# The second batch's q on float16 pairs instead of fp32, with the instruction orders planned anew

## The chip, the cores and the metric

The kernel runs on one core of a Trainium2 chip. A core has TensorE (matmuls, called PE in the profile, with its weight loads as PEld), VectorE (DVE), ScalarE (ACT), GpSimd (POOL) and SyncE (SP), which here issues the DMAs. Each engine works through its own queue of instructions and waits on semaphores for the others. The metric is the device time of one execution in microseconds, as a median of several runs.

## The reference

Four batches of eight heads go through an attention with random features; the result, as 2304 tokens of 512, goes through two feed-forward blocks. Cut to what is computed:

```python
# q, k, v: (4, 8, 576, 64), omega: (128, 64); q and k scaled by 64 ** -0.25
def phi(x):                       # 128 features of a row
    h = x @ omega.T - sum(x * x) / 2
    return exp(h - max(h)) / sqrt(128)
q_p, k_p = phi(q_s), phi(k_s)
kv = einsum('bhsm,bhsd->bhmd', k_p, v);  z = sum(k_p, axis=2)
num = einsum('bhsm,bhmd->bhsd', q_p, kv); den = einsum('bhsm,bhm->bhs', q_p, z) + 1e-6
x = (num / den)                   # as (2304, 512)
h = x @ w_in                      # 512 -> 2048
x = (h * sigmoid(1.702 * h)) @ w_out          # 2048 -> 512
out = ((x @ w_a) * (x @ w_b)) @ w_out2        # 512 -> 1536 -> 512
```

## The kernel before

**Numbers.** Most products are made from pairs of float16: a number is split into a high part (a scaled copy, ScalarE) and a low part (scaled number minus high part, VectorE), and a product is three f16 matmuls (high by high, high by low, low by high) added up in PSUM. The alternative is an fp32 matmul, which the trace shows as two records.

**Stages.** The tokens are cut into tiles of 512, one for each batch, and a fifth tile of what is left. The attention of batch 0 runs first, alone (0 to about 55 us, called the front below). Then comes the first feed-forward block, ffn1: for each of five tiles 16 column blocks `h` (L932-934, 12 matmuls of 512 columns), a gate (tanh on ScalarE, L941, or Silu; VectorE L944 and L954; ScalarE L953), and the products with w_out, `y` (L967-969). The attention of batch 1 is woven into ffn1 of tile 0, that of batch 2 into ffn1 of tile 1, and that of batch 3 into tile 2's and 3's. The first gate of tile t is called th`t`_0; in the profiled execution it stands at 65.08 us for tile 0, 180.31 us for tile 1, 274.17 us for tile 2. From about 500 us on ffn2 runs.

**Attention of one head pair.** For k and for q: rows are loaded (L625, L629), transposed, multiplied by omega (`project`), the row sums of squares are taken (ScalarE, L700), and the exponential is taken on ScalarE (L724) after a maximum on VectorE (L758). In batch 0 the transposition is on TensorE (L658, L662), and the transposed tiles `xt` and `xm` are copied out of PSUM by L667 (VectorE) or L669 (ScalarE), chosen by `EVX`. In later batches the rows are split to f16 (`x16`, L680 on ScalarE, L681 on VectorE) and transposed by DMA. Then k's features are multiplied by v to `kv`. In batches 0 and 1 this is fp32, with a copy by ScalarE (L822).

**The features of q.** In `qphase` they have to be transposed once more before they meet `kv`. With `f32=True` (batches 0 and 1 before) nine fp32 transposes on TensorE (L839) go to PSUM, ScalarE copies them out (L841), and ten fp32 products follow (L846). With `f32=False` (batches 2 and 3) the features are split to f16 pairs (`e16`, L734 on ScalarE, L735 on VectorE), one DMA transposition per head pair (L852) makes `eqT`, and 30 f16 products follow (L862-864), with `kv` as a pair too (`kv_parts`, L782 its low part). The result is normalised (L871-876) and becomes the next x tile: in batch 0 by TensorE transposes and two casts (L900 ScalarE, L901 VectorE), later by split and DMA transposition.

**Weights.** The 34 chunks of 1 MB of all weights come as raw 64-bit words, `wraw0` to `wraw33` (L478, on SyncE). VectorE puts each together in three passes (L492, L532, L540), makes sums for ffn2's chunks (L526), ScalarE makes the high parts (L550), VectorE the low ones (L499). This runs beside ffn1.

**Order.** The program is written as generators that are stepped in turn, but the final order on TensorE, VectorE, ScalarE and SyncE is the table `ORDER`, a compressed list of positions for each of the four engines. Where a DMA waits in SyncE's queue, all later ones wait with it.

Forty-five matmuls on a tile `idle` (L1403) are fillers with no result.

Of the kernel before, what the change touches and what calls it, by code (L numbers as in the profile page):

```python
# [25 lines left out]
S_KV = 2.0**2  # L26
# [7 lines left out]
    "eNqt3buua9uyGNZf2bjxCdjrRVKZASsXYMCJoMBwpMROBCeG/12ztyLn2ufeK8OBgz2x15ocfIxeg4tsVb3q//6X//Qf/+U//PWf"  # L34
    "H//46/zjr/jHX/mPv+off/U//pp//PX8x1+vf/z1/vnV/fXPX5yfvzk/f3Xu3/3c/vwccH6OOD+HnJ9j4ud2ce/n5+/j5+/j5+/j"
    "/v3PsfFzbPwcGz/H5s/t8ud2eR/w53b5c7v8uV3+3C5/bpc/t8uf29XP7erndvVzu7rP7Od29XO7+rld/dyufm5XP7frn9v1z+36"
    "53ZzH7vvA/Z9xL4P2e/7HO6Tm/vs7k36Pr35+dH35f7c/N6wf+77HnVvf29+b/38+fPz/vnntvNz27nn5uf28/P383PM/Pzu+XPb"
    "573tzx0/f273/Lnd8+d2z3sSf27z+vn96+f3r5/fv35+//r5/evn96+f37/uWb63+bmf98/t3j+3e//c7v1zu/fP7d4/t3v/3O79"
# [272 lines left out]
def fused_kernel(  # L311
# [13 lines left out]
    nc = tc.nc  # L325
# [4 lines left out]
    P = 128  # L330
# [1222 lines left out]
```

## Time and profile before

| | us |
|---|---|
| median of 3 runs | 876.65 (875.93 to 878.49) |
| profiled execution | 876.83 |
| its span | 874.9 |
| TensorE busy | 862.9 (99%) |
| weight loads | 628.8 (72%) |
| VectorE | 671.0 (77%) |
| ScalarE | 456.1 (52%) |

The span is the stretch of the profiled execution from its first to its last instruction; the execution's own time is 1.9 us longer. Shares are averages over stages that differ. TensorE's records overlap, so that a run of short ones is read by the distance of their starts and not by their drawn lengths.

### The profile page before, as it was taken

Reading aid. Unit: us, or ns where it says so; the run is one execution under the profiler, and the core shown is the slowest. Engines: PE = TensorE matmul, PEld = TensorE weight load, DVE = VectorE, ACT = ScalarE, POOL = GpSimd, SP = SyncE. Lnnn points to the kernel's source line nnn. Section 1 sums busy time; section 2 is a strip of 40 time slices with the busy share of each in tenths; the row PEclk is TensorE's granted clock in tenths of the full one; section 3 lists DMA queues with packets and bytes.
Section 4 is the critical chain, followed back from the end, with each engine's and each line's share of the span. In section 5 each row is a group of like instructions: output and inputs, shape, how many; then the busy total and the mean of one; then the engine's idle time right before and its main releaser. Section 6 shows DMA issues by size and latency. Waiting matters only on the chain.

```text
span 874.9 us, 17363 instructions
## 1 busy us (share of the span) xinstructions
PE 862.9 (99%) x7094; PEld 628.8 (72%) x7094; DVE 671.0 (77%) x1212; ACT 456.1 (52%) x1088; POOL 1.4 (0%) x10
## 2 busy tenths in 40 slices
PE   8999999999999999999999999999999999999997
PEld 6865655645555555544458888889988889888896
DVE  4889999999977877799211389978999558556756
ACT  6787785787667776564232554454543213233221
POOL 0000000000000000000000000000000000000000
PEclk9999999999999999999999999999999999999999
DMA  7947896673766215647110035422432112223312
GB/s 194 256 133 218 203 225 187 181 178 104 189 143 147 35 35 99 146 147 274 49 49 2 25 133 181 150 51 85 147 120 85 25 21 92 78 108 122 79 50 73
DMA packets 129343, 105.35 MB, mean 120 GB/s; under 512 B 97776, under 2 KB 111088, under 8 KB 127216
## 3 DMA queue, kind: packets, MB, share of 16 engines
q1 hardware_dynamic: 128558, 103.66, 41.8%
q8 instruction: 55, 0.90, 0.4%
q10 hardware_dynamic: 706, 0.59, 0.2%
q14 instruction: 24, 0.20, 0.1%
HBM read 71.07 MB, written 17.69 MB: 101 GB/s over the span
## 4 chain that ended last, share of the span: by engine, by line
PE 81%; DVE 10%; ACT 3%; issue 1%; DMA 1%; SPq 0%; ACTq 0%; DVEq 0%
PE y L968 6%; PE y L967 6%; PE y L969 6%; PE ph L932 6%; PE ph L934 6%; PE ph L933 6%; PE oA L1187 3%; PE oA L1189 3%; PE oA L1188 3%; PE paA L1091 3%; PE pbA L1091 3%; PE paA L1092 3%; PE pbA L1092 3%; PE pbA L1093 3%; PE paA L1093 3%; DVE wf L540 2%
## 5 line engine op out<-in xcount | busy, mean ns | idle before, releaser
L968 PE MATMUL y<-gl,w_out 128*128 128x512 f16 (+1 forms) x320 | 114.4, 358 | 0.7 <-DVE gl L954 0.7
L969 PE MATMUL y<-gh,w_out 128*128 128x512 f16 (+1 forms) x320 | 114.4, 358 | 0.0
L967 PE MATMUL y<-gh,w_out 128*128 128x512 f16 (+1 forms) x320 | 112.3, 358 | 0.0
L954 DVE SCALAR_TENSOR_TENSOR gl<-th,gh 128x512 f16<-128x512 f32 (+1 forms) x80 | 50.4, 633 | 67.8 <-ACT gh L953 67.6
L932 PE MATMUL ph<-xT,w_in 128*128 128x512 f16 x256 | 97.0, 379 | 1.4 <-ACT xT L900 0.8
L933 PE MATMUL ph<-xT,w_in 128*128 128x512 f16 x256 | 97.0, 379 | 0.9 <-DVE xT L901 0.9
L934 PE MATMUL ph<-xT,w_in 128*128 128x512 f16 x256 | 97.0, 379 | 0.3 <-DVE w_in L499 0.3
L1091 PE MATMUL paA<-forms,w_a 128*128 128x256 f16 (+1 forms) x240 | 61.0, 262 | 0.5 <-DVE ca L1112 0.5
L1091 PE MATMUL pbA<-forms,w_b 128*128 128x256 f16 (+1 forms) x240 | 61.2, 262 | 0.0
L1093 PE MATMUL pbA<-forms,w_b 128*128 128x256 f16 (+1 forms) x240 | 61.2, 262 | 0.0
L1092 PE MATMUL pbA<-forms,w_b 128*128 128x256 f16 (+1 forms) x240 | 61.1, 262 | 0.0
L1092 PE MATMUL paA<-forms,w_a 128*128 128x256 f16 (+1 forms) x240 | 61.0, 262 | 0.0
L1093 PE MATMUL paA<-forms,w_a 128*128 128x256 f16 (+1 forms) x240 | 61.0, 262 | 0.0
L1187 PE MATMUL oA<-w_o,ab 128*128 128x256 f16 x216 | 58.9, 273 | 0.3 <-DVE o L1195 0.3
L1189 PE MATMUL oA<-w_o,ab 128*128 128x256 f16 x216 | 58.9, 273 | 0.0
L1188 PE MATMUL oA<-w_o,ab 128*128 128x256 f16 x216 | 58.9, 273 | 0.0
L1101 ACT COPY ka<-paA 128x512 f32<-128x512 f32 (+1 forms) x30 | 16.3, 545 | 79.4 <-PE paA L1093 79.4
L953 ACT ACTIVATE gh<-th 128x512 f16<-128x512 f32 (+1 forms) x80 | 47.1, 589 | 14.8 <-DVE th L944 13.7
L1195 DVE SCALAR_TENSOR_TENSOR o<-oA,o 128x512 f32<-128x512 f32 (+1 forms) x45 | 28.4, 632 | 33.3 <-PE oA L1189 33.3
L934 PEld LDWEIGHTS <-w_in 128*128 128x128 f16 x320 | 31.3, 98 | 28.9 <-issue 1.2
L969 PEld LDWEIGHTS <-w_out 128*128 128x128 f16 x320 | 31.4, 98 | 28.8 <-issue 1.2
L933 PEld LDWEIGHTS <-w_in 128*128 128x128 f16 x320 | 31.4, 98 | 28.4 <-issue 1.4
(211 smaller groups left out, 2371.4 us busy)
## 6 DMA issues: line engine op xcount, KB each, us to landing
wraw<-in_moe_w_out_dram SPq DMA_DIRECT2D x14, 1024.0 KB
forms<-fd SPq DMA_DIRECT2D x8, 1792.0 KB
wraw<-in_moe_w_in_dram SPq DMA_DIRECT2D x8, 1024.0 KB
fd<-forms SPq DMA_DIRECT2D x4, 1792.0 KB
wraw<-in_moe_w_a_dram SPq DMA_DIRECT2D x6, 1024.0 KB
wraw<-in_moe_w_b_dram SPq DMA_DIRECT2D x6, 1024.0 KB
vt<-in_v_dram SPq DMA_DIRECT2D x16, 256.0 KB
rawq<-in_q_dram SPq DMA_DIRECT2D x16, 256.0 KB
```

Source lines behind the costliest of these rows:

```text
L932: nc.tensor.matmul(ph[:, :n], w[:, 0, c, fs], xh(c), start=(c == 0), stop=False)
L933: nc.tensor.matmul(ph[:, :n], w[:, 0, c, fs], xl(c), start=False, stop=False)
L934: nc.tensor.matmul(ph[:, :n], w[:, 1, c, fs], xh(c), start=False, stop=(c == KC - 1))
L967: nc.tensor.matmul(o, w[:, 0, f % 4, cs], gh[f][:, :n], start=(f == 0), stop=False)
L968: nc.tensor.matmul(o, w[:, 0, f % 4, cs], gl[f][:, :n], start=False, stop=False)
L969: nc.tensor.matmul(o, w[:, 1, f % 4, cs], gh[f][:, :n], start=False, stop=(f == FC1 - 1))
L1091: nc.tensor.matmul(o[:, i], wh, xh, start=first, stop=False, skip_group_check=True)
L1092: nc.tensor.matmul(o[:, i], wh, xl, start=False, stop=False, skip_group_check=True)
L1093: own["pe"] = nc.tensor.matmul(o[:, i], wl, xh, start=False, stop=final, skip_group_check=True).ins
L1187: nc.tensor.matmul(bank[:, t], lh, wh, start=first, stop=False, skip_group_check=True)
L1188: nc.tensor.matmul(bank[:, t], lh, wl, start=False, stop=False, skip_group_check=True)
L1189: nc.tensor.matmul(bank[:, t], ll, wh, start=False, stop=final, skip_group_check=True)
```

## The change

The code differs in five small places, beside the table.

```diff
@@ constants
-    VT, FILL, EVX = 4, 40, "q"
+    VT, FILL, EVX = 4, 40, ('k0_0', 'k0_1')
@@ features
-                if nm[0] in EVX:
+                if nm in EVX:
                     own["xt", nm] = nc.vector.tensor_scalar(out=o, in0=i, scalar1=S_QK, ...)
                 else:
                     own["xt", nm] = nc.scalar.activation(out=o, in_=i, func=AF.Copy, scale=S_QK)
@@ kphase32, fp32 branch
-        nc.scalar.copy(own["kv"][:, hp], pk)
+        if b:
+            kv_parts(hp, pk, S_KV)
+        else:
+            nc.scalar.copy(own["kv"][:, hp], pk)
@@ qphase, fp32 branch
-                cp = nc.vector.tensor_copy if gi in EVD else nc.scalar.copy
+                cp = nc.vector.tensor_copy if nm in EVD else nc.scalar.copy
@@ front
         for hp in range(2, NHP):
             a_load(att, "k", 0, hp)
+        w_load(0)
         w_steps(START_W, NW1)
@@ batches 1 to 3
-            begin_q(b, att, x1, psp_att, t0 + NHP * AL, AL, b == 1)
+            begin_q(b, att, x1, psp_att, t0 + NHP * AL, AL, False)
@@ ORDER (280 lines of base64)
-    "eNqt3buua9uyGNZf2bjxCdjrRVKZASsXYMCJoMBwpMROBCeG/12ztyLn2ufeK8OBgz2x15ocfIxeg4tsVb3q//6X//Qf/+U//PWf"
+    "eNpdu3uOK9uyINZf2bj2MTjjRVKeALXfgAA5jTYEWe1ITkOOoH9XzRFkrb1vXxmHp3YVk4/MyFzkiJgR/8+//ef/9G//01//5fGv"
```

So in batch 1 q's features are split to f16 pairs and transposed by DMA; k stays fp32, and its result is made a pair. The `EVX` edit moves batch 0's copies of four q tiles (`xt` and `xm`) from VectorE to ScalarE, and those of `k0_0` and `k0_1` from ScalarE to VectorE. `EVD` is empty, so that edit changes nothing. The load of chunk 0 of the weights goes in SyncE's queue ahead of q's rows of batch 0 instead of behind them. Below, line numbers of the changed kernel stand one to four above those of the kernel before.

TensorE, the first products of the second batch's q (`q1_0`), behind the projections of its last head pair (`xt_q1_3`), in the kernel before:

```order
L693 LDWEIGHTS xt_q1_3_1517
L693 MATMUL pa_1660<-om_l_94,xt_q1_3_1517 128x128
L846 MATMUL pa_1699<-kv32_128,eT32_q1_0_1579 128x65 x5
L967 LDWEIGHTS w_out2_91
L967 MATMUL y0_0_1009<-gh0_10_1904,w_out2_91 128x512
```

and now:

```order
L693 LDWEIGHTS xt_q1_3_1526
L693 MATMUL pa_1664<-om_h_93,xt_q1_3_1526 128x128
L866 LDWEIGHTS eqT_q1_0_1595
L866 MATMUL pa_1704<-kvh_97,eqT_q1_0_1595 128x65
L867 LDWEIGHTS eqT_q1_0_1595
L867 MATMUL pa_1704<-kvl_98,eqT_q1_0_1595 128x65
L868 LDWEIGHTS eqT_q1_0_1595
L868 MATMUL pa_1704<-kvh_97,eqT_q1_0_1595 128x65
```

The five fp32 products of one head have become f16 products, three for each.

VectorE, the last instructions ahead of tile 1's first gate, before (`wf` are weight chunks being put together, `w_a0` a finished one of ffn2, `k2` rows of batch 2):

```order
L526 TENSOR_TENSOR sx17_3458<-wf17_2815,sx17_3458 128x256
L532 SCALAR_TENSOR_TENSOR wf18_3545<-wraw18_2614,wf18_3545 128x1024
L710 TENSOR_REDUCE sq_k2_0_2237<-rawk_2_0_1212 128x9
L681 SCALAR_TENSOR_TENSOR x16_k2_1_2264<-rawk_2_1_1326,x16_k2_1_2264 128x9x64
L797 SCALAR_TENSOR_TENSOR v16_k2_1_2618<-vm_134,v16_k2_1_2618 128x2x65
L681 SCALAR_TENSOR_TENSOR x16_k2_2_2322<-rawk_2_2_1440,x16_k2_2_2322 128x9x64
L710 TENSOR_REDUCE sq_k2_1_2269<-rawk_2_1_1326 128x9
L499 SCALAR_TENSOR_TENSOR w_a0_2610<-wf17_2815,w_a0_2610 128x512
L499 SCALAR_TENSOR_TENSOR w_a0_2610<-wf17_2815,w_a0_2610 128x256
L499 SCALAR_TENSOR_TENSOR w_a0_2610<-sx17_3458,w_a0_2610 128x1024
```

and now:

```order
L493 TENSOR_SCALAR wf16_2313<-wraw16_2174 128x1024
L909 TENSOR_TENSOR x16_q1_3x_2118<-xf_q1_3_2029,x16_q1_3x_2118 128x512
L493 TENSOR_SCALAR wf17_2879<-wraw17_2202 128x1024
L911 TENSOR_TENSOR x16r_96<-xf_q1_3_2029,x16r_96 64x128
L798 SCALAR_TENSOR_TENSOR v16_k2_0_2537<-vm_134,v16_k2_0_2537 128x2x65
L682 SCALAR_TENSOR_TENSOR x16_k2_0_2296<-rawk_2_0_1213,x16_k2_0_2296 128x9x64
L798 SCALAR_TENSOR_TENSOR v16_k2_1_2682<-vm_134,v16_k2_1_2682 128x2x65
L798 SCALAR_TENSOR_TENSOR v16_k2_1_2682<-vt_133,v16_k2_1_2682 128x2x260
L711 TENSOR_REDUCE sq_k2_0_2301<-rawk_2_0_1213 128x9
L533 SCALAR_TENSOR_TENSOR wf16_2313<-wraw16_2174,wf16_2313 128x1024
```

Before, chunk 17 was split and 18 half put together here; now it is chunk 16 that is half put together, and 17 has only begun.

ScalarE, around the last casts of the first x tile (`xT0`) and the first gate `th0_0`, before:

```order
L680 ACTIVATE x16_k1_2_972<-rawk_1_2_820 128x9x64
L900 CAST xT0_100<-pa_729 128x512
L680 ACTIVATE x16_k1_3_1062<-rawk_1_3_823 128x9x64
L906 CAST x16r_96<-xf_q0_3_738 64x128
L900 CAST xT0_100<-pa_761 128x512
L724 ACTIVATE e32_k1_0_855<-pa_923,nb_k1_0_1_949 128x128 x4
L550 ACTIVATE w_in0_87<-wf2_841 128x4x256
L941 ACTIVATE th0_0_914<-ph0_0_844 128x512
```

and now:

```order
L904 CAST xT0_100<-pa_763 128x512
L681 ACTIVATE x16_k1_2_972<-rawk_1_2_820 128x9x64
L701 ACTIVATE rawk_1_1_817,sq_k1_1_910<-rawk_1_1_817 128x64 x2
L945 ACTIVATE th0_0_914<-ph0_0_844 128x512
L945 ACTIVATE th0_1_939<-ph0_1_862 128x512
L551 ACTIVATE w_in0_87<-wf4_921 128x4x256
L957 ACTIVATE gh0_0_917<-th0_0_914 128x512
L957 ACTIVATE gh0_1_942<-th0_1_939 128x512
L725 ACTIVATE e32_k1_0_855<-pa_923,nb_k1_0_1_949 128x128 x4
L945 ACTIVATE th0_2_981<-ph0_2_885 128x512
L681 ACTIVATE x16_k1_3_1062<-rawk_1_3_823 128x9x64
```

The splits of batch 1's k rows, `x16_k1_2` and `x16_k1_3`, stood ahead of a cast each; now the last cast is ahead of both, and `x16_k1_3` comes after the third gate.

## Rows read from the trace of the kernel before

**Rows 1.** Page, part 1: engine, busy us, share of the span, instructions.
```profile
PE 862.9 (99%) x7094; PEld 628.8 (72%) x7094; DVE 671.0 (77%) x1212; ACT 456.1 (52%) x1088; POOL 1.4 (0%) x10
```

**Rows 2.** Stretches: length, busy PE, PEld, DVE, ACT, POOL; clock, DMA share, GB/s.
```profile
0.00:20.00 20.00, 17.31 (x124) 13.48 (x125) 9.26 (x25) 12.79 (x35) 1.38 (x10) 0.91 0.71 181
...
60.00:80.00 20.00, 19.14 (x110) 9.46 (x110) 19.84 (x36) 15.58 (x57) 0.00 (x0) 1.00 0.55 154
80.00:100.00 20.00, 20.00 (x137) 12.25 (x137) 19.97 (x32) 15.10 (x56) 0.00 (x0) 1.00 1.04 259
...
240.00:260.00 20.00, 20.00 (x171) 11.07 (x170) 14.32 (x40) 13.73 (x39) 0.00 (x0) 1.00 0.71 153
```

**Rows 3.** Timeline of PE in batch 1's stage: start us, drawn us, instruction.
```profile
130.60 1.23 PE L846 MATMUL pa<-kv,eT_q 128*128 128x65 f32 x10
131.66 0.38 PE L969 MATMUL y<-gh,w_out 128*128 128x512 f16 x1
131.88 0.38 PE L967 MATMUL y<-gh,w_out 128*128 128x512 f16 x1
```

**Rows 4.** Timeline of PE elsewhere, then PEld's group of the f16 products' loads.
```profile
43.01 1.04 PE L839 MATMUL pa<-ident,e_q 128*128 128x128 f32 x8
43.88 0.93 PE L1403 MATMUL idle<-om_h 128*128 128x256 f16 x7
...
258.91 0.19 PE L862 MATMUL pa<-kvh,eqT_q 128*128 128x65 f16 x1
...
259.78 0.20 PE L864 MATMUL pa<-kvh,eqT_q 128*128 128x65 f16 x1
...
L863 PEld LDWEIGHTS <-eqT_q 128*128 128x128 f16 x80 | 7.4, 98 | 1.0 <-issue 0.4
```

**Rows 5.** Groups by line and form, VectorE: busy us, mean ns | idle before.
```profile
L532 DVE SCALAR_TENSOR_TENSOR wf<-wraw,wf 128x1024 int32<-128x1024 int32 x34 | 41.3, 1215 | 0.2
L492 DVE TENSOR_SCALAR wf<-wraw 128x1024 int32<-128x1024 int32 x34 | 23.3, 684 | 1.4 <-DMA wraw<-in_moe_w_in_dram 1.1
L526 DVE TENSOR_TENSOR sx<-wf 128x256 f32<-128x256 f32 x36 | 14.1, 416 | 0.1
L735 DVE SCALAR_TENSOR_TENSOR e_q<-e_q,e_q 128x512 f16<-128x512 f32 x16 | 11.0, 686 | 1.2 <-ACT e_q L734 1.2
L499 DVE SCALAR_TENSOR_TENSOR w_a<-sx,w_a 128x1024 f16<-128x1024 f32 x6 | 7.3, 1218 | 0.0
L782 DVE SCALAR_TENSOR_TENSOR kvl<-pa,kvh 128x130 f16<-128x130 f32 x8 | 2.3, 285 | 0.0
L735 DVE SCALAR_TENSOR_TENSOR e_q<-e_q,e_q 128x128 f16<-128x128 f32 x8 | 2.1, 268 | 0.0
```

**Rows 6.** The same view of ScalarE.
```profile
L734 ACT ACTIVATE e_q<-e_q 128x512 f16<-128x512 f32 x16 | 10.3, 643 | 1.8 <-PE pa L808 1.8
L841 ACT COPY eT_q<-pa 128x512 f32<-128x512 f32 x16 | 9.2, 586 | 5.4 <-PE pa L839 5.4
L669 ACT ACTIVATE xt_k<-pa 128x512 f32<-128x512 f32 x4 | 2.5, 613 | 0.7 <-PE pa L658 0.6
```

**Rows 7.** Waits of PE (us, times, longest), then ScalarE's timeline with [idle before].
```profile
PE ph L933 <- DVE xT L901: 0.9, 1, 0.9
PE ph L932 <- ACT xT L900: 0.8, 1, 0.8
...
59.89 0.68 ACT L680 ACTIVATE x_k<-rawk 128x576 f16<-128x576 f32 x1 [1.17 <-DMA rawk<-in_k_dram]
```

**Rows 8.** One DMA transposition of q in SyncE's timeline, and the stretch around it.
```profile
252.73 3.29 SPq L852 DMA_TRANSPOSE eqT_q<-e_q  x1
...
252.50:256.50 4.00, 4.00 (x27) 1.90 (x24) 3.60 (x9) 2.48 (x6) 0.00 (x0) 1.00 0.81 122
```

**Rows 9.** The first q rows: asked for by SyncE, transposed by PE (timelines).
```profile
12.43 0.60 SPq L625 DMA_DIRECT2D rawq<-in_q_dram  x1
...
19.62 0.61 PE L658 MATMUL pa<-ident,rawq 128*128 128x128 f32 x4
```

More of the change, by code (lines that the diff above doesn't have):

```diff
@@ L33 @@
 ORDER = (
-    "eNqt3buua9uyGNZf2bjxCdjrRVKZASsXYMCJoMBwpMROBCeG/12ztyLn2ufeK8OBgz2x15ocfIxeg4tsVb3q//6X//Qf/+U//PWf"
[L35 to L38, printed above, removed]
@@ L219 @@
[L219 to L222 removed]
+    "eNp13buOK9uyINZf2bj2MTjjRVKeALXfgAA5jTYEWe1ITkOOoH9XzRFkrb1vXxmHp3YVk4/MyFzkiJgR/8+//ef/9G//01//5fGv"
@@ new lines @@
+    "v86//op//ZX/+qv+9Vf/66/511/Pf/31+tdf758/3T///OL8/Ob8/Or8/C5+7n/u/342ip+/x882+bNp/Nwvfu4XP/eLn/vlz9/y"
+    "5355H/zn0c/9373f3e7n5/j5Oe+2P9vlz3b5s13e5+z7mPfB+j5a34fr+7xzn2zuq537EHMfYzzx3WLuFnO3mLvF3C2ed4vn3eL5"
+    "s0X9/Ff9/Efdn+/b/dmsfravn43qZ+v62a5+Nuuf+/XP/frnfv1zv/65z33G+5ruq7mvo3+2ff5sd1/i827z87/Xzzb35b1+trkv"
+    "7r62+9LuK7sv7L6u+7Luq9oXdd/B876D530HTzvwvoPnfQf3YeN138F94Hjd93wf+r6Vu+Xd8G73ui/lHrSfje7dz+Pn5t77PH5u"
+    "Xj/3ev389XWP6b3Hz6O+f+7w/nnM98/f3z+P9P65z/vnUd4/93v/3O99D76jfw/zo+7NDYLHPYKPvjc3Hh43IB73fsJEfNwAOTcq"
@@ new lines @@
+    "zoaJm/taHP17+M89vkdQiaoUSvevN5DOjY5zQ+PcWDrh8e6db1idG1PnBtTZiLr3u4f03GN6SoT53d3iBtdJP92HKv/pUe6D3mg4"
+    "5Q/3dyXy7u/uoT/32J978M890ueGwLnH/9wDfsTk3bNxd37c/Rsvoe8P96FuAJwbAeeGwLkxcG4QnBsFp93FyXWf7UbFuSFxnja7"
+    "h/oepLhHKd7+88bKPVBxj9S5B/vcCDkO+Y2Q45g//afT9d7Fa7kPdZ7+atv7qp7Oave7T3nfzLlv5ngzDrwnfzjL75PfOAhH/8bJ"
+    "uYFy3q4JN1Bv0J37Ss99pee+0nNfadzYiBsH4YJxPJTnuDvsxlA8XFXuwzv3b2zEjY24IRXhmuEP934uM64zLjSuQDfWwnXFheUG"
+    "TdxQiRtckS449w8uUzcs4oZF3LCIGzlRrkf3r+V395FvRMTb/e5/3qCJGzRxAy5uNEW5SrkGOlB327fLn+vfvQDePZl3J+bdiXl3"
@@ new lines @@
+    "Yt6dmPbBDbO4YRY3wqL94V4L737Ju1/yuIzeR7n7L+/+y/s+0rXTxTPc3M3uLsm7D9LV1WXYddiFeK/E936utfcd5X1Hed9R3h2R"
+    "d0dkeXiPcp/jHpk8frpPdI9M3iOT93jkPQAZrvMewL8G934uq3cflH1wz5m80Z73rKiHC/J9jhvtOX6y7b3f3fd5z5m8gZk3MPMG"
+    "ZrY/eND7h3tG5Xjk9/3dvaLfHVsPT34v6Hcn1nHpv9d+e+2ePXnPnrxnT93dVHc3VbrLfYD9F8nNvfM9j/Ie6Wxv5r7me9yy/St2"
+    "H7S9vrvFPQfzns55T7q853Teky6fnty/d/f13aNQ9yiUo3BP4rwncd5TstI/U366O+w+b93nLc97z+l8+52/3nfuzdyXUfdl1N3j"
+    "dXdY2WF339fd2XWfqF5+8s/d/bftHoq6D1oe1Cu4+77s+3ti59vz3vfx9rv7Pm7I1w3MuoFZN1TqhkrdUKnjr/dl3FApofL2z/x9"
@@ new lines @@
+    "Xv8ev/zDe+9393Pfo9r3MPY9jH0PYz/8wQP41/s+243xujFeN0TrngF1z4C6Z0Af/4Lff8K9NP/o3/Du45/z+wf/eQ93373bNyz6"
+    "Hvi+B77vkel7ZDrd727mo8Dd2X13dvs0cPdz3/3cdz+3TwZ3P/d+Xrhb3Gjv+97KZw4fOPaTx33NThIfPG7Il48e98j0PQB9933d"
+    "RynnzPjPu9n4yHI3E/c34OoGXL98RrmvyqF1QH32uUFYT5927qPcICxBeM+F2o8wdzfdI133SPf9aR4++9wPL/egzD0o8/CfPgi9"
+    "7yeex73x2educXfxiIO3m/tsN1RKqLx9xhJ1NnOk77Z73O6+8rsbPn3Dp48/3C1u+HT4YHaf6J61c8/auYdxHKgbFn3Dom9Y9A2L"
+    "vq++PXw4oPdRShw4Mt6gm/sGbfH2Ac7N/cONjblHa+7Rmnu05h6tuUdr7nk597ycGyDjw+INkLkBMjdA5h6F8UR3F48dew/t3KM1"
@@ new lines @@
+    "Lx8N74PeQzY+Rb7cxYu87+M+ed8n7/vk7UOqUPEx1efUGxt9Y6NvbPSNjb6x0Tc2WmzcOGifHI9PoOfe3A+Tx+/ux8m775/2/Q2V"
+    "vqHST//ps+59UKHyEqce4H4AvsfoeY/R8x6jp2N0j37fo/+8r/55T/bnPbee99x6lg+w9ynvWfYs97uPd8/L5432133Q133QV/hA"
+    "ez9Zh7/6wHsf9L7V532rT5+rfbC+b/XpM7K36n28HdX7Fm789Y2/EX9C7yFs76G4b2bu88593rnPOyE6Bdw9vg8Pej923/983ch5"
+    "hf+8H7JvrL1urD3v23/ew/18+919ffbG21/v67th9rqv9OWVelX3EjR3N73uC395oqeP7353d0n53d0v9yi87lF43Xh53Xh53bf6"
+    "8pRvn/Z93L+f9x9ey/2riL1HYe6+n3tk5u77KVF8/3CvZnOvZnOvZnOvZuMrje80+6XmvlJfa8of7mb3KMw9CnOPwtz3Nvcgz33N"
@@ new lines @@
+    "77uf33f/ve9V5f3wu/uV415QXjdKXuUn7/K+wRvjrxvez/uHpz/4duO43b02dzfN3U3z9DXrvqC7m+bpZHJnO8fpd7d4++lucffG"
+    "vJ2hvpr5bnZjyL66mz0d7vtyn/flPu/LfXq592R/3ZP91b6D2e0OwP2db1M3mt5OjYeb+47upeB1w+Lly9c96d73pHu93Ngb99uX"
+    "O+93tvumfWu7J+zbCes0CN8F70u78fe88fe88fcUfwIunXT3zaQvjXeLdNLdLdJ5ee939/PzhsXTzr7v7dm+Xt773ff29EX3xsbz"
+    "xsbzxsbzxsZznJL3qB4v8sZa+mJ5f5feoJ/uLrlP+U77xU/3rd4gfLs8+BZ7j+DzHsHnPYLPewSfrjQ3xp++AN9j+fS19+V7793i"
+    "7qb3PWHf94R936h7u6q8nHn3D+UP96WVL733Fdy4et+4et8d8b479n137Pvu2Pfdse+7Y993x77Dc9z7pXd5D+MNkNcNkNcNkNcN"
@@ new lines @@
+    "kJcAeQhWLHCP+T14r3vwXndvvI4r3N3i7ojXDZXXfdCXB73772X/3SPzvkfmfY/Mu/3O1/W77d27r/TTfRTXjbtPX3efvu4+fd03"
+    "/SoQcJ+3RKwAvve7x/I9Hvm+y/3P+3j3+L5gxv3r6x7fl6vy/vU+2z33X/e0f93T/nVP+9c97d/3kL1fXvPda/eJ3gLkPsD7PvL7"
+    "PvL7Psr7PsrbZuN+9xXch3rfi8f7nuLve4q/7yn+fgIKW9w73wB5L1bcn26AvG+AvG+AvG+AvJ1RL6ZBKx4LJFzjwUhckJxfgoSL"
+    "ODfJCBpxNsMRX3ofqx/LH491Eg9LOx5nH5aaLJYsngCRB9940JAH5nicvXVPLPLgIg+e8gAqD6LyACSP2EdzHyjygCQPNvLAKQ9E"
+    "8gAgj9z7eMbce/q59v6enW88WMlj9vcen3Y8ahnIYzKWB914gIQHU3j03nqE9oyM44FjHuzlMStJ/Oextxho9yeReDz3Z4/ANx5r"
@@ new lines @@
+    "WoTjsaxFLB7I4sEsHrWv3G3ta/YIVOeBdR5c5wF2Hr3vwj2BzAPBPOjJg8Q8gMkDyDyIx2NNbGOAfKC2s0z2IS3H7mNhjt1q2HLY"
+    "Y/YWiD32louJlhWgx8tzIZylmlWbFZv1sTWlRaW1syWzJbT1svWzx4b9a1+5d/f2LKjm8d53Z0++94js+/LKl/XW8BbxVvGW8dbx"
+    "7KVlq/WtVSSMdBaiVqKWotai0NKhLmfRaNVo2ejsK3nvu7CtCF/9WzBcBFwFXAZc7lvvW/Bb7FvtW+5bK1wsXC1cLlwbXDVcE1wU"
+    "XBVcFlwXXBhcGVwVxEYn9mdnAbw+GOZwmMNRDqc5oObkcua+L1stLzLvA70P9T7Y+3DvA74P+T7o+7DvA7YO2Tqx4rlxJbaXF1cG"
+    "1y8B5lmFXIZchzwbmbPbbux5Pbm3XpX9ia8Oqzq5MfPcW4/5WhD2mM7ZVcZlRop2MNrBb4d0HdR1cuPNWba+CBjPCuPKJJU8WPJw"
@@ new lines @@
+    "ybMwCRYPWTxo8bDFAyFPbNZCJHPIAx0PdTzY8XDHAx5PLGavZjt/Y3V6j6z3i3QO0zlQ53ClQ91OLGTv0Re3uXj92j3g914P1zuo"
+    "7UDCQwkPQToI6TCkE6vhq+OiKBbJ9xk/nO51Ojsg5eGaB2wesnm45QGXh0MeynNyZV1EIanDpA6UOrDyoKDDgg4MOjTo4KCDeA7j"
+    "OQDwEMBTe9RctWRqjlTNkas5kjVHtuZI1xz5kRP7ru1nKZITG5P2vyzJid2fXq1EyYl9tRtvrkiU/mD6w+nPQj1oP7FXJHsASx54"
+    "dZjVqc1PvPd2kw5u7UlqcwDdIXQH0R0yd2oTCI4mnDt07uC5g7QOIzuQ7NC5g+dO7bvYPXz21rt47+1mSLyX956VziB7Gzqf/ORY"
+    "HBGPD2wPsT3I9tTe2le471C5ww4PZTuY7YC6Q+oOOzxo8SC/w/wOUDpE6RDJg/IOyzsw79C803u+b5pmr1quM7lJmr3OuFYA6pN7"
@@ L223 @@
+    "bx/ePrx9ePvw9uHtw9uHtw9vH94+vH14+/D24e3D24e3D28f3j68fXj78Pbh7cPbh7cPbx/ePrx9ePvw9uHtw9uHtw9vH94+vH14"
     "+/D24e3D24e3D28f3j68fXj78Pbh7cPbh7cPbx/ePrx9ePvw9uHtw9uHtw9vH94+vH14+/D24e3D24e3D28f3j68fXj78Pbh7cPb"
@@ L307 @@
+    "TQH4HPrJLPgkOt8EwvPD9t8cg08q9eV+Xzl6kwQ+vjw+CYTXJ3nw3mTCN9fi35DYHMm3Jtm/5/1bypufQuG9oDw+6Yn38x8lvflb"
+    "HezsddpGfjMRn+j6LVeefxTefq45v2W+j28Ww+F1RvdvqsCFyLnrMuQq5CLkGrRphvwtKn7+Vha/v/kH16E/GQYn9J+K4a0J/i3Q"
+    "dWlxHXFJcS35U9zrQvLvq4Ofv/of/8gS/Kn//ZMW2OLeb1rgY/5f0N9ryvO3KtkF5T8sEX59EwRbGPz4WP5eHJi12HJMHcrV/y/t"
+    "bwpANS/f/1Pw+6euV3biP6rmdUr+R7XDW2P8+Eq/U865tifgN08R8fyv/+//B4bH+ag="
 )
```

481 lines of the change are left out of this document (218 added, 263 removed).

## The prediction

> **What bounds the kernel now.** I read the page's totals first [rows 1]. TensorE's matmuls cover 99% of the span, its weight loads 72%, VectorE 77% and ScalarE 52%. A row of matmuls can be covered and still stall, since their drawn durations overlap, so the second view is the table by stretches [rows 2]. From 60 to 100 us, where the change's second batch is worked on, two engines are full together: VectorE 19.8 and 20.0 us of 20, TensorE 19.1 and 20.0 us, while weight loads fall to 9.5 and 12.3. Which of them sets the pace is told by the step from one matmul to the next in the timeline of the same stage [rows 3]: a 512-column matmul begins 0.22 us after the one before it, and 512 columns at the granted clock of 1.00, the 2.4 GHz level, are 0.213 us. There is no gap between steps there. TensorE is the bound, and VectorE runs along just full. The reader should take from this that work removed from TensorE's queue shortens the kernel one for one, provided VectorE's queue shrinks as much in the same stage. The third view, the waits, shows what else may be won: few waits of TensorE are near 1 us, two of them on the casts of the first x tile [rows 7].
>
> **TensorE's work.** The second batch's q is four head pairs. Before, each has ten fp32 products. The timeline has ten records, five products, between 130.60 and 131.66 [rows 3], so 1.06 us for five; the four pairs hold eight such fives, 8 x 1.06 = 8.5 us. Each pair also has nine fp32 transposes; eight of them run from 43.01 to 43.88 [rows 4], 0.109 us each, so 36 are 3.9 us. Both go. In their place stand 30 f16 products per pair, 120 in all. The third batch's, which have this form already, begin at 258.91 and the thirtieth at 259.78 [rows 4]: 0.87 us for 29 steps, 0.030 us each, 3.6 us for 120. The sum is 8.5 + 3.9 - 3.6 = 8.8 us less on TensorE. In the order shown, the five fp32 products become a run of f16 products at the same place, directly behind the projections of the fourth head pair, so nothing else is opened up there.
>
> The Trainium skill, page "TensorE: Matmul & The Clock Gate", section "Back-to-back issue gap", says that a stream of weight-load and matmul pairs at 128 columns is spaced about 81 ns, because the load counts in the spacing. By that the 120 would take an estimated 9.7 us and the edit would save only 2.7. The same instructions here step at 30 ns [rows 4], each with its own weight load, so the measured step is used.
>
> **VectorE.** Added in the stage: eight 512-wide e-splits of 0.686, four 128-wide of 0.268 and four kv splits of 0.285 [rows 5], 5.5 + 1.1 + 1.1 = 7.7 us. That would make VectorE the bound if nothing left. But the new order moves weight conversions. The snippets show that before the first gate of tile 1 (th1_0) VectorE had already finished chunks 16 and 17 and begun 18; now it has only begun 16 and 17. Put off: four 1.215 passes (second pass of 17 and 18, third of 16 and 17), one shift of 0.684, eight sums of 0.416 and two 1.218 splits of sums [rows 5], 4.9 + 0.7 + 3.3 + 2.4 = 11.3 us, smaller splits not counted. And one shift and five instructions of 1.215 (passes of chunks 3 and 4, a split of w_out) that used to follow the first gate of tile 0 now precede it by VectorE's order, 0.684 + 5 x 1.215 = 6.8 us. Between th0_0 and th1_0 VectorE therefore has 7.7 - 11.3 - 6.8 = -10.4 us, more than the 8.8 that TensorE loses. The put-off work lands after 180 us, where ffn1 of tile 1 and 2 runs: VectorE is at 14.3 of 20 us by 240 us [rows 2], so 5.7 us are free in each such row and hide it. If that cover were missing, the 7.7 us would show.
>
> **The front, before th0_0.** VectorE must take the 6.8 us there. It does 9.3 us of work in the first 20 us [rows 2] and waits for loads otherwise, so the room exists, but the weights must have landed. That is what the load of chunk 0 ahead of the q rows is for or against; see the rivals. ScalarE takes over the copies of four q tiles and gives two of k to VectorE: 2 x 0.613 [rows 6], and with the 64-row mates, taken at half, 1.8 us more on ScalarE in batch 0, and as much less on VectorE. TensorE waits for such a copy on either engine. Bounds for ScalarE's extra: nothing (it is idle 7 of the first 20 us [rows 2]) to 1.8 (all of it on TensorE's path, as its exponentials gate the products). I take half, +0.9. In the stage of batch 1 ScalarE gains eight splits of 0.643 and loses eight copies of 0.586 [rows 6], +0.5, off the path.
>
> **The wait for xT0.** Two waits of TensorE, 0.9 and 0.8 us [rows 7], end with the casts of the first x tile. The ScalarE row at 59.89 [rows 7] shows why: a split of batch 1's k stood idle 1.17 us for its rows from DRAM, and the last cast stood behind it in the queue. In the new order both k splits (x16_k1_2, x16_k1_3) come after the last cast, one of them even after three gates. I take both waits as gone, -1.7; the bounds are 0 (the cast is late for another reason, its transposes) and -1.7. What is late next is the tile's own weights, which come earlier by the new order.
>
> **The DMA queue.** SyncE issues four more transpositions. One of the third batch's, at 252.73, takes 3.29 us to issue, and the 4-us stretch around it has a DMA share of 0.81, 3.2 us [rows 8]; four make 13 us of all 16 DMA engines. At 80 to 100 us the share is 1.04 already [rows 2], elsewhere less. A product that waits for its transposition holds TensorE. In the order shown, TensorE reaches q1_0's products only behind all of q1_3's projections, and the last split of q1_0 stands on VectorE some 20 us of its work earlier, an estimate from the order and the durations in [rows 5]; for the last pair the distance is about 11 us. I price this at 0, bounds 0 to 13. Queued behind each transposition on SyncE are the next weight chunks, which the deferral above makes less urgent.
>
> **Sum.** 876.83 (the profiled execution) - 8.8 - 1.7 + 0.9 = 867.2. It ran 0.18 above the median shown, so 867.0 in the median's terms.
>
> **The rivals.**
> *Chunk 0 ahead of q costs the front.* Its 1 MB now goes before the q rows. At 181 GB/s [rows 2] 1.05 MB take 5.8 us. The rows of q were asked for at 12.43 and used by TensorE at 19.62 [rows 9]; with about 7 us between, a shift of 5.8 eats the room and can idle TensorE in the front. Against: TensorE has fillers and k's work there, and the order moves q's use too. Time: 867.0 + 5.8 = 872.8. Chance 0.12.
> *VectorE is the bound (other side, slower).* VectorE is full from 60 to 100 us [rows 2] with TensorE only as long as it feeds it. If the put-off conversions come back as late weights before ffn2, the 7.7 us less the 1.8 given to ScalarE are paid in full, and TensorE's saving is hollow: 876.65 + 5.9 = 882.6. It decides if TensorE waits for VectorE's e-splits or gates in 60 to 180 us. Against it stands the unbroken 0.22 us step [rows 3]. Chance 0.06. The Trainium skill, page "Perfetto Trace Analysis", section "Identifying the Most-Contended Engine", says that matmul busy share is no good measure and weight-load busy share is; by it TensorE, at 9.5 to 12.3 of 20, would have room and VectorE would be the most contended engine. The step in the timeline speaks against that reading here, which is why the chance is small.
> *The DMA queue.* All 13 us of transpositions on the path: 876.65 - 8.8 + 13 = 880.9. Chance 0.03.
> *Nothing comes of it.* The saving on TensorE is filled by waits for VectorE, whose queue was full: 876.65. Chance 0.04.
> *Weight loads limit the f16 products.* Each of the 120 brings a load of 98 ns [rows 4]. Were loads not hidden behind the products, 120 x 0.098 = 11.8 us would come for the 12.4 that go: with the other terms as they are, 867.0 + 11.8 - 3.6 = 875.2. The 0.030 step is against it; the page on TensorE's issue gap, of the Trainium skill, points this way. Chance 0.02.
>
> **How the numbers follow.** The forecast, 867.0, has 0.73. Its own range comes from the bounds: without the xT0 term and with all of ScalarE's 1.8 it is 869.6 plus a little for late weights, 870.5; with nothing for ScalarE 866.1, and if other waits of the front go as well as the 0.9-us pair did, to 862.5. To hold 8 in 10 it has to reach into the first rival, so 862 to 874. Within 0.3% of 876.65 is 874.0 to 879.3, about what a measurement of this kernel can tell from no change. Faster than that: the forecast and the front rival, 0.73 + 0.12 = 0.85. Same: nothing comes of it and the weight loads, 0.04 + 0.02 = 0.06. Slower: VectorE and the DMA queue, 0.06 + 0.03 = 0.09.
>
> **What would show it.** In the profile after: 72 fewer fp32 records of products and 36 fewer transposes, 120 more f16 products at 0.030; th1_0 about 10 us earlier, of which th0_0 has 1; the two waits on xT0 gone; VectorE still about full from 60 to 170. The forecast is wrong if TensorE shows waits of over 1 us on q's DMA transpositions, on VectorE's e-splits, or in the first 30 us on the q rows, or if 512-column steps after 60 us exceed 0.22.

## The result, and the profile after

| | before | after |
|---|---|---|
| median of 4 runs, us | 876.91 (875.93 to 878.49) | 867.79 (866.64 to 868.39) |
| ratio to before | | 0.9893, 95% interval 0.9875 to 0.9911 |
| profiled execution, us | 876.83 | 868.39 |
| its span, us | 874.9 | 866.3 |

The kernel before had a fourth run here. The change makes the kernel 1.07% faster. The prediction was 867.0 us, with 862 to 874 as its range.

The page's totals after, which answer to [rows 1]: engine, busy us, share of the span, instructions.

```profile
PE 854.5 (99%) x7098; PEld 620.5 (72%) x7098; DVE 680.9 (79%) x1224; ACT 459.0 (53%) x1092; POOL 1.4 (0%) x10
```

TensorE is 8.4 us shorter, VectorE 9.9 us longer, and the shares hardly move; they don't tell where the time went. The view by stretches does, cut at the first gate of each tile. The kernel before, from th0_0 to th1_0 and from there to th2_0 (columns as in [rows 2]):

```profile
65.08:180.31 115.23, 113.89 (x706) 65.75 (x705) 113.07 (x200) 84.44 (x269) 0.00 (x0) 1.00 0.76 207
180.31:274.17 93.86, 93.51 (x733) 50.41 (x732) 86.48 (x201) 66.12 (x167) 0.00 (x0) 1.00 0.62 144
```

The changed kernel, the same two stages:

```profile
65.06:170.27 105.21, 104.31 (x708) 56.56 (x707) 103.86 (x196) 80.12 (x264) 0.00 (x0) 1.00 0.82 209
170.27:267.75 97.48, 96.00 (x742) 51.34 (x741) 92.54 (x207) 71.19 (x176) 0.00 (x0) 1.00 0.64 144
```

The front, up to th0_0, took 65.08 us and takes 65.06: between these two profiles nothing is won there. The first stage, with the second batch's attention, is 10.0 us shorter. TensorE's busy time fell by 9.6 us in it and VectorE's by 9.2, so that both still fill it. The second stage is 3.6 us longer. The rest (th2_0 to th3_0 at 274.17 to 375.03 before, 267.75 to 366.71 now, and what follows) gives 2.2 us again. Together 8.6 us.

The f16 products now stand in stage 1 too; in TensorE's timeline the first, the second and the last of the 30 of head pair 1, answering to [rows 4] (start us, drawn us):

```profile
147.28 0.19 PE L866 MATMUL pa<-kvh,eqT_q 128*128 128x65 f16 x1
147.31 0.19 PE L867 MATMUL pa<-kvl,eqT_q 128*128 128x65 f16 x1
...
148.15 0.20 PE L868 MATMUL pa<-kvh,eqT_q 128*128 128x65 f16 x1
```

They run from 147.28 to 148.15, 0.030 us apart, right behind each other. If each of TensorE's matmuls is given the step of its form as the timelines show it (512 columns 0.2155 us, 256 columns 0.109, 128 columns 0.0555, 65 columns 0.030, fp32 records 0.105 to 0.112, those of 130 columns 0.215), stage 1 adds up to 113.0 us of TensorE work before and 103.0 now, and the whole kernel to 853.4 and 844.0. I call this estimate TensorE's own work below; a stage's length less this is what it stood still. It stood still 2.2 us in stage 1, before and after.

The waits of TensorE after (us in total, times, longest), answering to [rows 7]:

```profile
PE pa L663 <- DMA rawk<-in_k_dram: 2.9, 2, 1.5
PE idle L1458 <- DVE warm L1460: 1.1, 1, 1.1
PE pa L693 <- ACT e_q L725: 0.9, 1, 0.9
PE pa L693 <- DVE kvl L783: 0.7, 1, 0.7
PE pa L807 <- ACT e_q L725: 0.5, 1, 0.5
```

The two waits on xT0's casts are gone. The longest now is for the very first rows of k. None is on q's rows or on a DMA transposition of q: products of head pair 0 begin at 136.52, 13.7 us behind the issue of their transposition, those of pair 3 at 156.7, 7.4 us behind.

### The profile page after: what moved, and what is told of

Read it like the earlier page. It is cut to its first block, busy times and chain, and to the rows that moved or that the text cites. A ratio compares the mean times of both kernels' runs of the same rounds, so it can differ in the third digit from the quotient of the medians.

```text
span 866.3 us, 17393 instructions
## 1 busy us (share of the span) xinstructions
PE 854.5 (99%) x7098; PEld 620.5 (72%) x7098; DVE 680.9 (79%) x1224; ACT 459.0 (53%) x1092; POOL 1.4 (0%) x10
## 4 chain that ended last, share of the span: by engine, by line
PE 93%; DVE 3%; DMA 2%; ACT 1%; issue 0%; SPq 0%; ACTq 0%
PE y L971 7%; PE y L973 7%; PE y L972 7%; PE ph L936 6%; PE ph L938 6%; PE ph L937 6%; PE oA L1191 3%; PE paA L1095 3%; PE pbA L1095 3%; PE pbA L1096 3%; PE paA L1097 3%; PE paA L1096 3%; PE pbA L1097 3%; PE oA L1193 3%; PE oA L1192 3%; PE pa L693 1%
## 5 line engine op out<-in xcount | busy, mean ns | idle before, releaser
L973 PE MATMUL y<-gh,w_out 128*128 128x512 f16 (+1 forms) x320 | 113.1, 358 | 0.0
L971 PE MATMUL y<-gh,w_out 128*128 128x512 f16 (+1 forms) x320 | 109.8, 358 | 0.0
L938 PEld LDWEIGHTS <-w_in 128*128 128x128 f16 x320 | 31.3, 98 | 28.4 <-DVE w_in L500 0.4
L1105 ACT COPY kb<-pbA 128x512 f32<-128x512 f32 (+1 forms) x30 | 16.3, 542 | 66.7 <-PE pbA L1097 64.2
L973 PEld LDWEIGHTS <-w_out 128*128 128x128 f16 x320 | 31.2, 98 | 28.3 <-DVE w_out L500 0.2
L972 PEld LDWEIGHTS <-w_out 128*128 128x128 f16 x320 | 31.3, 98 | 28.1 <-issue 0.4
```

Source lines behind the costliest of these rows:

```text
L938: nc.tensor.matmul(ph[:, :n], w[:, 1, c, fs], xh(c), start=False, stop=(c == KC - 1))
L971: nc.tensor.matmul(o, w[:, 0, f % 4, cs], gh[f][:, :n], start=(f == 0), stop=False)
L972: nc.tensor.matmul(o, w[:, 0, f % 4, cs], gl[f][:, :n], start=False, stop=False)
L973: nc.tensor.matmul(o, w[:, 1, f % 4, cs], gh[f][:, :n], start=False, stop=(f == FC1 - 1))
```

## The experiments

For the variants the order table was rewritten: each instruction kept its place in one of the two orders (taken from that kernel's trace), and a new one was put where the text says. Line numbers of the variants differ a little from those above.

### Which engine paces stage 1

Three kernels take work off one engine alone. The first takes matmuls out of the kernel before:

```diff
-                nc.tensor.matmul(o, w[:, 0, f % 4, cs], gl[f][:, :n], start=False, stop=False)
+                if j or not 3 <= f < 14:
+                    nc.tensor.matmul(o, w[:, 0, f % 4, cs], gl[f][:, :n], start=False, stop=False)
```

> The kernel before, without 44 of TensorE's 512-column products in stage 1 (low part of the gate by w_out, blocks 3 to 13 of tile 0, left out), nothing else touched: 44 x 0.2155 = 9.5 us less on TensorE between 83 and 162 us, VectorE's work as it was. Theory (TensorE paces stage 1 and its saving counts one for one also without a new order): 876.5 - 9.5 = 867. Rival (VectorE, at 112.7 of 115.2 us, stops the saving after 2.5 us): 872 to 874.

The other two take passes off VectorE, from the kernel before and from the changed one:

```diff
-            nc.vector.scalar_tensor_tensor(
+            if i not in (5, 6, 7, 8, 9, 10, 11, 12, 13):
+                nc.vector.scalar_tensor_tensor(
                     out=fs[i], in0=staged[i][:, :, :, 0], scalar=29, in1=fs[i], ...
```

> The kernel before without the second pass of weight chunks 5 to 13 (it leaves out the lowest three bits of these weights), 10.9 us less on VectorE in stage 1, nothing moved. Theory (TensorE bounds the stage): at most TensorE's 2.2 us of standing still there go, 874 to 876. Rival (VectorE, busy 112.7 of 115.2 us, bounds it): 866 to 870.

> The changed kernel without the second pass of weight chunks 5 to 13 (it leaves out the lowest three bits of these weights), nine instructions of 1.215 us, 10.9 us less on VectorE in stage 1. Theory (in the changed kernel TensorE bounds stage 1, VectorE costs only the single waits in it): 866 to 867.8, at most the 2.2 us that TensorE stands still between th0_0 and th1_0. Rival (VectorE bounds the stage): 10 us faster, 857 to 860.

Measured, as ratios to before: 1.0001 (0.9984 to 1.0017) for the kernel before with less TensorE work, 0.9993 (0.9983 to 1.0003) for the kernel before with less VectorE work, 0.9904 (0.9889 to 0.9918) for the changed kernel with less VectorE work, where the changed kernel itself had 0.9893 (0.9875 to 0.9911). None of the three gains on the kernel that it was made from. Their stage 1 in the view by stretches, in this order, each from its own trace:

```profile
64.04:178.37 114.33, 107.61 (x662) 60.96 (x661) 113.05 (x200) 84.35 (x270) 0.00 (x0) 1.00 0.79 210
```

```profile
64.68:178.86 114.18, 113.50 (x706) 65.72 (x705) 104.17 (x191) 84.20 (x269) 0.00 (x0) 1.00 0.80 210
```

```profile
63.91:168.94 105.03, 104.24 (x708) 56.59 (x707) 95.26 (x187) 79.76 (x264) 0.00 (x0) 1.00 0.83 209
```

With TensorE's own work at 103.5 us and VectorE at 113.05, the stage of the kernel before lasts 114.3. With TensorE at 113.0 and VectorE at 104.2, it lasts 114.2. So both engines bound the stage of the kernel before, each at 113, and taking 9.5 us off TensorE or 8.9 off VectorE alone shortens the stage by 1 us and the kernel by nothing that can be measured. In the first of the three, TensorE's longest waits are for ScalarE's exponentials:

```profile
PE pa L676 <- ACT e_q L708: 1.9, 4, 0.8
PE pa L676 <- ACT e_k L708: 1.2, 3, 0.6
```

ScalarE in turn waits there for VectorE (6.8 us in gates, 1.6 us before exponentials), and VectorE itself waits only 0.7 us in all. My theory for this run (TensorE's saving counts one for one without a new order) fell; its rival was nearer, but still expected a gain of 2.5 us or more. The second run was forecast rightly, by the theory that TensorE is the bound; only the first shows that VectorE is one as well.

In the changed kernel 8.6 us more off VectorE shorten the stage by 0.2 us, no more than this stage differs between profiles (105.2 to 105.5 us in four kernels that have it alike), so TensorE alone holds it at 105. Whether VectorE's 103.9 us would do so too is not shown: no run takes work off TensorE in the changed kernel. A stage with 113 us of work on each of two engines can become 10 us shorter only if both queues shrink. That shrinking both is also enough is not shown apart from the new order: no run takes both off the kernel before.

### The edit and the order apart

The changed kernel with batch 1's q back on fp32 (and k's result again one copy by ScalarE), everything else in the new order:

```diff
-            begin_q(b, att, x1, psp_att, t0 + NHP * AL, AL, False)
+            begin_q(b, att, x1, psp_att, t0 + NHP * AL, AL, b == 1)
```

> The changed kernel with its new order, but batch 1's q on fp32 again (transposes on TensorE, copies by ScalarE, ten fp32 products per head pair) and k's result as one copy; everything else stays where the new order has it. Theory (the gain is TensorE work that left stage 1): TensorE gets its 9 us back, th1_0 falls near 180 us again, total 867.8 + 9 = 877 us. Rival 1 (the gain is in the new order, fewer waits): it stays at 868 to 870. Rival 2 (VectorE is the bound): with 7.7 us less on VectorE in the stage it gets faster than the changed kernel, 861 to 866.

It took 895.6 us, ratio 1.0228 (1.0212 to 1.0244). TensorE's own work in stage 1 is 112.3 us, 9.3 more than in the changed kernel, as the theory has it; but the stage lasts 134.2, not the 115 that the theory had:

```profile
64.34:198.50 134.16, 122.76 (x704) 70.42 (x703) 100.27 (x180) 80.46 (x264) 0.00 (x0) 0.94 0.53 147
```

TensorE waits, and its granted clock averages 0.94. If that mean is made of 1.00 and 0.50, some 16 us of the stage ran at 0.50, which takes up to 8 us from TensorE, an estimate. Its timeline in a place with the fp32 transposes (brackets: idle before, and what ended it):

```profile
178.53 0.61 PE L824 MATMUL pa<-ident,e_q 128*128 128x128 f32 x4
179.87 0.66 PE L824 MATMUL pa<-ident,e_q 128*128 128x128 f32 x4 [0.73 <-ACT eT_q L826]
181.20 0.33 PE L824 MATMUL pa<-ident,e_q 128*128 128x128 f32 x1 [0.68 <-ACT eT_q L826]
```

Each group of transposes waits for ScalarE to copy the one before out of PSUM; these tiles come from a pool of two banks that the projections use too. The groups were put in behind each other by me, so how much of this belongs to fp32 and how much to their places stays open. The run is slower for these other reasons, so it can't decide the rival with VectorE alone; the relief of the changed kernel above does.

The kernel before with the f16 edit alone, in its old order, and the same with VectorE's passes of chunks 5 to 13 left out as above:

```diff
-            begin_q(b, att, x1, psp_att, t0 + NHP * AL, AL, b == 1)
+            begin_q(b, att, x1, psp_att, t0 + NHP * AL, AL, False)
```

> The kernel before, with its order, and only the f16 edit of batch 1's q put in: e-splits directly behind the exponentials, the DMA transposition behind them, the f16 products where the fp32 ones stood. No weight work is put off. VectorE had 112.7 us of work in the 115.2 us between th0_0 and th1_0; it now has 120.4. Theory (TensorE and VectorE bound the stage together, and the saving needs the deferral of weight work): stage 1 as long as VectorE's work, 120 to 121, total 877 + 5 = 882, or about 876 if half of VectorE's idle time elsewhere takes it up. Rival (TensorE alone is the bound): 877 - 9 = 868.

> The f16 edit in the order of the kernel before (as in the second experiment, which took 889.9 us), without the second pass of weight chunks 5 to 13 (lowest three bits of these weights left out): the same order, 10.9 us less on VectorE in stage 1. Theory (VectorE's overfull queue is what the edit alone lost): stage 1 from 129.5 down to 108 to 114, total 870 to 876. Rival (latency of the DMA transpositions or wrong places): above 883.

They took 889.94 us, ratio 1.0166 (1.0149 to 1.0183), and 889.98 us, 1.0161 (1.0143 to 1.0179). The edit alone makes the kernel slower, as expected of the first, but by 14 us instead of 5. And 9.6 us less on VectorE change the stage by 1.5 us and the time by nothing, so its full queue is not what the 14 us are; my theory for the second fell. Stage 1 of the two:

```profile
64.44:193.91 129.47, 111.00 (x710) 58.40 (x709) 121.74 (x218) 85.63 (x269) 0.00 (x0) 0.96 0.79 205
```

```profile
64.23:192.24 128.01, 110.98 (x710) 58.57 (x709) 112.09 (x209) 85.71 (x270) 0.00 (x0) 0.96 0.81 208
```

The first row shows that weight work has to leave the stage: with the old weight plan VectorE has 121.7 us of work between the gates, more than the whole stage took before. But in the second VectorE is idle for 16 us and TensorE for 17. Most of TensorE's waiting is for the two parts of the gate:

```profile
PE y L958 <- ACT gh L944: 5.1, 2, 2.9
PE y L959 <- DVE gl L945: 4.6, 3, 2.9
```

In both the granted clock averages 0.96, by the same reckoning some 10 us at 0.50. A part of the chain of waits of the second (start us, us, what) shows one reason why VectorE is late:

```profile
134.25 0.39 SPq L843
...
134.74 1.30 SPq L674
...
136.09 5.61 DMA wraw<-in_moe_w_out_dram
...
141.72 0.70 DVE wf L479
```

A weight chunk is asked for behind two DMA transpositions in SyncE's queue (L843 that of q's features, L674 that of q's rows), and VectorE begins it when it lands; VectorE waits 5.4 us for such chunks in the stage. This is the mechanism of my rival on the DMA queue. It shows in the old order, which asks for chunks late, and not in the new one. What else makes the gates late in the two kernels I have not taken apart.

Then I moved only the weight work to where the new order has it, with fp32 and with f16 (no line of code but the order table changes):

> The kernel before, fp32 for batch 1's q, with only its weight work moved to where the new order has it. Theory (stage 1 of the kernel before is bound by TensorE at 113 of 115 us, so less VectorE work there gives nothing): 875 to 878, stage 1 113 to 116. Rival (the new weight order is itself the gain): 867 to 870.

> The f16 edit put into the order of the kernel before (as in the second experiment), and in addition all weight work (loads, VectorE's passes, sums and splits, ScalarE's high parts) moved to where the new order has it between the gates. Theory (the edit alone overfills VectorE in stage 1, the deferral is what makes it pay): stage 1 shrinks from the 129.5 us of the edit alone to 105 to 112, total 868 to 875. Rival (what is lost with the edit alone are the places of the other instructions, not the weight work): it stays above 883.

They took 914.8 us, ratio 1.0444 (1.0428 to 1.0459), and 917.91 us, 1.0476 (1.0446 to 1.0506). Both theories and both rivals missed. Already th0_0 comes at 77 us, 12 us late. TensorE has single waits of 1.9 and 2.8 us there for VectorE's copies of q, and its granted clock averages 0.85 and 0.81 from 20 to 65 us. I put the waits down to conversions that run early in the new order and now stand ahead of attention work that is still at its old place; that is argued, not tested. The weight plan is not a part that can be carried over alone; so I could not show that the deferral by itself is what pays.

### The front

The changed kernel with chunk 0 of the weights asked for behind the q rows again. Only SyncE's order in the table changes; no line of code does, and the other three engines keep their orders.

> The changed kernel with the load of weight chunk 0 back behind the q rows in SyncE's queue; nothing else touched. Theory (the early load costs the front nothing, since fillers and k's work cover q's rows; it lets VectorE begin chunk 0 at 21 us instead of 29): the same or up to 2 us slower, 867.5 to 870. Rival (chunk 0 ahead of q delays the front by up to its transfer time of 5.8 us): faster, 862 to 866.

It took 881.45 us, ratio 1.0081 (1.0049 to 1.0113), with eleven runs from 879.67 to 890.76. That is 13 us slower than the changed kernel between the profiles, far beyond what I expected. The rival had forecast a gain, and there is none; but the run moves the load against an order of VectorE and ScalarE that counts on it, so it does not price the load by itself. Its rows on VectorE, ScalarE and TensorE:

```profile
25.80 0.69 DVE L479 TENSOR_SCALAR wf<-wraw 128x1024 int32<-128x1024 int32 x1 [7.74 <-DMA wraw<-in_moe_w_in_dram]
...
29.12 1.06 ACT L537 ACTIVATE w_in<-wf 128x1024 f16<-128x1024 f32 x1 [6.63 <-DVE wf L527]
...
30.39 2.07 PE L663 MATMUL pa<-om_f,xt_q 64*128 64x128 f32 x12 [6.09 <-ACT kv L812]
```

In the new order VectorE takes chunk 0 at 21 us and ScalarE its high part before the next copy of kv. When the chunk comes 5 us later, all three engines stand behind it. And the loss is twice the wait, as the stretches show (columns as in [rows 2]; the third number from the end is TensorE's granted clock):

```profile
22.00:24.00 2.00, 2.00 (x21) 2.00 (x20) 0.00 (x0) 0.50 (x2) 0.00 (x0) 1.00 1.05 380
...
28.00:30.00 2.00, 0.00 (x0) 0.00 (x0) 2.00 (x3) 0.88 (x1) 0.00 (x0) 0.50 0.19 59
...
40.00:42.00 2.00, 2.00 (x12) 1.78 (x11) 1.39 (x3) 2.00 (x7) 0.00 (x0) 0.50 0.00 0
...
52.00:54.00 2.00, 2.00 (x14) 2.00 (x13) 0.00 (x0) 1.62 (x5) 0.00 (x0) 0.68 1.25 299
54.00:56.00 2.00, 2.00 (x17) 1.53 (x15) 1.91 (x7) 1.40 (x3) 0.00 (x0) 1.00 1.00 391
```

The clock falls from 1.00 to 0.50, the 1.2 GHz level, while TensorE waits, and stays there until 53 us although TensorE is busy nearly all the time. So th0_0 comes 13.1 us late for a wait of 6.1. The other 7 I put down to the clock: no other wait of over 1 us is new in this front.

The changed kernel with the copies back on their old engines:

```diff
-    VT, FILL, EVX = 4, 40, ('k0_0', 'k0_1')
+    VT, FILL, EVX = 4, 40, "q"
```

> The changed kernel with the copies of batch 0's transposed tiles on the engines of the kernel before (q's four on VectorE, k0_0 and k0_1 on ScalarE), each at the same time as it now has. Theory (ScalarE paid half of 1.8 us): 867 within 1 us, 866.5 to 868. Rival (the whole 1.8 us of ScalarE are on the path): 866. Other rival (VectorE has no room for 2 us in the front): 868.5 to 870.

868.79 us, ratio 0.9909 (0.9886 to 0.9933): it can't be told from the changed kernel. The ratios differ by 0.0016, or 1.4 us, with an uncertainty of 2.6 us by the two intervals, so my +0.9 is neither shown nor refuted.

### What stage 2 gives back

> The changed kernel without the second pass of weight chunks 16 to 20, five instructions, 6.1 us less on VectorE, four of them where the put-off weight work now lies (169 to 267 us). Theory (the put-off work makes VectorE full in stage 2 and brings two waits of TensorE at 212 and 229 us): those 1.8 us go, 866 us. Rival (the waits are latencies of batch 2's attention, not VectorE's fullness): 867.8, the waits stay.

> The changed kernel with 16 of TensorE's 512-column matmuls of h and y moved ahead of the four places where it waits for batch 1's or 2's attention (106.7, 131.4, 212.4 and 229.6 us, waits of 0.9, 0.3, 0.7 and 1.1 us), so that it works through the wait. Theory (these waits are latencies that other matmuls can cover): 2 to 2.9 us faster, 864.5 to 866. Rival (the engines waited for are late by their own queues, and the wait comes back at the next place): 867 to 868.

The first leaves out the second pass of chunks 16 to 20 (`if i not in (16, 17, 18, 19, 20)` at the place shown above), the second only moves matmuls in TensorE's order. They took 866.75 us, 0.9901 (0.9886 to 0.9916), and 869.36 us, 0.9912 (0.9888 to 0.9935); both are the changed kernel's time. With 4.4 us less of VectorE work in stage 2 (88.1 instead of 92.5) TensorE still stands still 2.5 us there instead of 2.8, and the waits that I had put down to VectorE's fullness stay:

```profile
PE pa L680 <- ACT e_q L712: 1.0, 1, 1.0
PE pa L794 <- ACT e_q L712: 0.4, 1, 0.4
```

So they come from the chain of batch 2's attention (exponentials on ScalarE), and my theory fell. Working through them, as the second kernel does, doesn't help either, and its theory fell too; in it new waits stand a little later, one on a gate and one on kv's low part:

```profile
214.95 0.81 PE L957 MATMUL y<-gh,w_out 128*128 128x512 f16 x3 [0.54 <-ACT gh L943]
...
216.98 0.22 PE L679 MATMUL pa<-om_h,xt_q 128*128 128x128 f16 x1 [0.69 <-DVE kvl L769]
```

No version of these beats the changed kernel.

## Why the prediction was right, point by point

**The bound.** I read TensorE as the bound from its unbroken step, with VectorE "along just full", and made the gain hang on the proviso that VectorE's queue shrinks as much in the same stage. The single reliefs show that the proviso was the heart of it, and that "TensorE is the bound" was half of the truth: before, both engines were the bound, and 9.5 us off TensorE alone gave 1 us of stage. Where I gave "VectorE is the bound" 0.06, the forecast held only because the order also takes 9.2 us of VectorE work out of the stage (10.4 forecast). A step without a gap between two matmuls does not tell that the engine is the only bound.

**TensorE's work.** 8.8 us less were forecast, 9.4 measured as its own work in the whole kernel; the f16 step is 0.030 as taken. The step of an fp32 record of a product is nearer 0.112 us than the 0.106 that one run of ten gave. The "72 fewer fp32 records of products" should have been 80, eight fives of ten records; with 80 the page's count comes out (7094 - 80 - 36 + 120 = 7098).

**VectorE's put-off work.** I let stage 2 hide it at no cost, with 5.7 us free in a row of 20. Stage 2 is 3.6 us longer. Of these, 1.9 are TensorE work that the new order moved there (92.7 us before, 94.7 now), and most of that comes back in the next stage, whose own work falls from 99.4 to 97.7; the prediction had no such term. The other 1.7 are more standing still. The relief shows that VectorE's fullness is not what these are, so a price of nothing for the put-off work itself is not refuted; the waits on batch 2's attention that came with the new order are what the sum left out.

**The front.** -1.7 for the casts and +0.9 for ScalarE were forecast; between the two profiles the sum is 0.0. The two waits are gone as forecast, and the longest wait is now for k's first rows. But the length of the front also goes with the granted clock, which I had left out: its mean over the first 20 us is 0.91 in both profiles, and other values in others. With the old front, th0_0 came at 65.08 us at 0.91, and at 64.04, 64.23, 64.44 and 64.68 at 1.00. With the new one, it came at 63.91, 64.34 and 65.06 at 0.91, at 65.61 at 0.83, and at 62.75 at 1.00. At like clock the new front is thus shorter by 0 to 1.9 us. The 0.8 forecast may be in there, but a single profile of each kernel can't size it.

**The rivals.** Chunk 0 ahead of q does not cost the front 5.8 us: TensorE has no wait on q's rows in it, and without the early load the new order loses 13. "Nothing comes of it" is what the first relief shows for the kernel before: 9.5 us off TensorE were filled by waits behind a full VectorE. The DMA queue is not on the path, with 7 to 14 us between a transposition and its products, but with the old order it is, in part. Weight loads do not space the f16 products, which step at 0.030 us.

**The sum.** -9.6 forecast; measured -8.6 in the span, and -9.1 between the medians. The stages: front 0.0, stage 1 -10.0, stage 2 +3.6, and -2.2 behind it. By its terms the forecast was 8.8 of work and 0.8 of waits; measured are 9.4 of work, while TensorE stands still 0.8 longer in all. So the work was right and 0.6 too small, the waits went the other way by 1.6, and that the total comes within 1 us is in part luck.

## What to carry to other kernels

When two engines are full in the same stage, test each one by leaving work out: here 9.5 us off one and 8.9 off the other each gave 1 us of stage, while the change, which takes 10 and 9 off both, gave 10. An edit that moves work between engines and an order made for it are one change: the edit in the old order cost 14 us, and one load put back in the new order cost 13. A wait has to be priced with the clock that it loses: here, in one run, a wait of 6 us came to 13.

## What the hardware showed that I had not expected

After a wait of 6.1 us TensorE's granted clock stayed at 0.50, the 1.2 GHz level, for some 23 us of nearly unbroken work (30 to 53 us), and the loss came to 13 us, of which I put about 7 down to the clock. In the two stages with the f16 edit in the old order, where TensorE was idle for a seventh of the time in many separate waits, the mean granted clock was 0.96; with q back on fp32 in the new order it was 0.94.
